# Six attention units with sums of exponentials on TensorE and a three-pass value product, and weight conversion in fewer, wider, moved steps

## The chip, the core and the metric

The kernel runs on one core of a Trainium2 chip. The metric is the device time of one execution in microseconds (us). The core's engines each run their own instruction stream in order and wait for each other through semaphores: PE (TensorE) multiplies matrices, DVE (VectorE), ACT (ScalarE) and POOL (GpSimd) work on rows, and SP issues the transfers. PEld is the loading of PE's stationary operand.

## What is computed

Three layers follow each other on x of shape 8 x 576 x 512. The change touches the first and the way in which weights of the second are prepared.

```python
def _attn_ref(q, k, v, phi):            # 8 batches, 8 heads, 576 rows, 64 columns, 32 memory slots
    a = phi - np.max(phi, axis=2, keepdims=True)
    a = np.exp(a)
    a = a / (np.sum(a, axis=2, keepdims=True) + 1e-09)
    k_m = np.einsum('bhsm,bhsd->bhmd', a, k)
    v_m = np.einsum('bhsm,bhsd->bhmd', a, v)
    scores = scale * np.matmul(q, k_m.transpose(0, 1, 3, 2))
    scores = scores - np.max(scores, axis=-1, keepdims=True)
    attn = np.exp(scores)
    attn = attn / (np.sum(attn, axis=-1, keepdims=True) + 1e-09)
    return np.matmul(attn, v_m)
def _moe_ref(x, w_tok1, w_tok2, w_ch1, w_ch2):
    xt = x.transpose(0, 2, 1)
    h = np.maximum(xt @ w_tok1, 0.0) @ w_tok2
    u = x + h.transpose(0, 2, 1)
    return u + np.maximum(u @ w_ch1, 0.0) @ w_ch2
```

A third layer (gated attention by four experts) ends the program. The weights `w_tok1`, `w_tok2`, `w_ch1`, `w_ch2` arrive as 64-bit floats.

## The kernel before

Products are made in three passes of fp32r matmuls: each operand is split into a high and a low part, and `mm3` adds high times high, high times low, and low times high. Plain fp32 matmuls (transposes, `s2k`, `s3`) stand as two records each in the trace.

**Units.** The attention layer and the token half of the second layer run in 16 units n (a batch and four of its heads), spread over a loop t = -3 to 15, so that in one turn unit t is in its last steps (`s4a`, `s4g`, `s4b`, `s4c`), unit t+1 in its scores (`s3`, `s3b`, `s3c`), unit t+2 in its memory products (`s2s`, `s2k`, `s2t`, `s2q`) and unit t+3 in its first softmax (`s1a`, `s1t`, `s1b`). `s2s` adds up the exponentials of a unit over its five row blocks on POOL (tile `es`); `s2k` multiplies them with keys and values (20 matmuls with 32-column weights, four heads side by side in the array), and one more matmul of `es` with a column of ones gives the sums over the partitions. `s2k` then builds `Vh` and `Vl`, the high and low values of four heads on a masked diagonal, and on POOL and ACT the doubled tile `Vd`, which holds each half of them twice. `s4a` transposes the attention weights and splits them into `aT` in four pieces of 64 partitions, high part of one pair of heads beside its low part; with the doubled values two matmuls then do what three passes do. `s4c` uses them, at 288 columns each, and adds the token product. DVE's `hl` of `s4b` (L435) follows the last matmul of `s4b`; its start is used as a mark of a unit below.

**Blocks.** From t = 2 on, PE's stream is filled up with the first three of twelve column blocks of the channel product (`block_1`, tiles `b`, `uh`, `ul`, `hh`, `hl`, `u`), 11 pieces for each turn.

**Weight conversion.** `f64_split` turns 64-bit words into a high and a low fp32r tile. For one piece that is ACT L119, DVE L120, L123, L124, L125, L127, ACT L128 and DVE L129. In the loop the pieces are the token weights (nine, 256 or 288 columns), three column blocks of the channel weights (six pieces of 512 columns, staging tiles `cst` of four buffers), and four more column blocks (`more_weights`, 16 pieces of 256 columns, two buffers). A second lot of ten 512-column pieces (`chload`) follows beside the last pieces of `block_1` and the first blocks of the channel stage (tiles `h`, `o`, `hh`, `hl` of L606 and L607).

**Order.** The framework schedules the instructions: it takes the written order as a wish and places each instruction on its engine by a timeline of its own. So the `wsome(w)` calls in the loop do not fix where a conversion step ends up.

Of the kernel before, what the change touches and what calls it, by code (L numbers as in the profile page):

```python
# [8 lines left out]
F32 = mybir.dt.float32  # L9
F32R = mybir.dt.float32r  # L10
I32 = mybir.dt.int32
AF = mybir.ActivationFunctionType
OP = mybir.AluOpType
AX = mybir.AxisListType
# [47 lines left out]
def fused_kernel(ctx: ExitStack, tc, q, k, v, phi, w_tok1, w_tok2, w_ch1, w_ch2,  # L62
# [26 lines left out]
    ones = consts.tile([128, 1], F32, name="ones")  # L89
# [20 lines left out]
    def f64_split(pool, stage, hi, lo, n, wd=512, nb=3):  # L110

        P = stage.shape[0]
        L, Hw = stage[:, :, 0], stage[:, :, 1]
        x = pool.tile([128, wd], I32, name="cx", bufs=nb)
        y = pool.tile([128, wd], I32, name="cy", bufs=nb)
        m = pool.tile([128, wd], F32, name="cm", bufs=nb)
        x_, y_, m_ = x[0:P, 0:n], y[0:P, 0:n], m[0:P, 0:n]

        ACT.activation(m_, Hw.bitcast(F32), AF.Abs, scale=REBIAS)  # L119
        DVE.tensor_scalar(m_, m_, LEAST, MOST, op0=OP.max, op1=OP.min)  # L120
        yield

        DVE.tensor_single_scalar(y_, L, 28, op=OP.logical_shift_right)  # L123
        DVE.tensor_scalar(y_, y_, 0.5, 7.0, op0=OP.mult, op1=OP.min)  # L124
        DVE.scalar_tensor_tensor(x_, m_.bitcast(I32), 3, y_, op0=OP.logical_shift_left, op1=OP.bitwise_or)  # L125
        yield
        DVE.scalar_tensor_tensor(y_, Hw, SIGN, x_, op0=OP.bitwise_and, op1=OP.bitwise_or)  # L127
        ACT.activation(hi, y_.bitcast(F32), AF.Copy)  # L128
        DVE.tensor_sub(lo, y_.bitcast(F32), f(hi))  # L129
        yield  # L130
# [69 lines left out]
    with ExitStack() as sa:  # L200
# [27 lines left out]

        units = [(b, g) for b in range(B) for g in range(2)]
        NU = len(units)  # L230
        et, kmT, Vh, Vl, ah, al, pmc, est, kst, ssb, aTt, gt_, ht, pmx, Vd = ({} for _ in range(15))

        def load_phi(n):
# [48 lines left out]
                load_phi(n + 2)  # L282

        def s2s(n):
            e = et[n]
            es = wk_.tile([128, 4, M], F32, name="es", bufs=1)
            e2 = wk_.tile([128, 4, 2, M], F32, name="es2", bufs=1)
            est[n] = es
            POOL.tensor_add(e2[:], e[:, :, 0:2, :], e[:, :, 2:4, :])
            POOL.tensor_add(es[:], e[:, :, 4, :], e2[:, :, 0, :])  # L290
            POOL.tensor_add(es[:], es[:], e2[:, :, 1, :])

        def s2k(n):
            e = et.pop(n)
            kv = kv_
            es = est.pop(n)
            p = pp.tile([128, 512], F32, name="g", bufs=2)
            for j in range(5):
                for h in range(4):
                    PE.matmul(p[32 * h:32 * h + 32, 0:128], lhsT=e[:, h, j, :],  # L300
                              rhs=kv[:, :, h, j, :], start=(j == 0), stop=(j == 4),
                              tile_position=(0, 32 * h))
            PE.matmul(p[:, 128:129], lhsT=es[:].rearrange("p h m -> p (h m)"), rhs=ones[:],
                      start=True, stop=True)
            r = wk_.tile([128, 1], F32, name="kr", bufs=2)
            DVE.tensor_scalar_add(r[:], p[:, 128:129], 1e-9)
            DVE.reciprocal(r[:], r[:])
            ks = wk_.tile([128, 2, 64], F32, name="ks", bufs=1)
            kst[n] = ks
            DVE.scalar_tensor_tensor(ks[:], p[:, None, 0:64].to_broadcast([128, 2, 64]), r[:],  # L310
                                     kmask[:], op0=OP.mult, op1=OP.mult)
            vm = wk_.tile([128, 64], F32, name="vm", bufs=1)
            ACT.activation(vm[:], p[:, 64:128], AF.Copy, scale=r[:])
            if n + 1 < NU:
                load_kv(n + 1)
            vmb = vm[:, None, :].to_broadcast([128, 4, 64])
            h_ = wk_.tile([128, 4, 64], F32R, name="Vh", bufs=3)
            l_ = wk_.tile([128, 4, 64], F32R, name="Vl", bufs=3)
            Vh[n], Vl[n] = h_, l_
            vh = wk_.tile([128, 64], F32R, name="vh", bufs=1)  # L320
            vl = wk_.tile([128, 64], F32, name="vl", bufs=1)
            POOL.tensor_copy(vh[:], vm[:])
            POOL.tensor_sub(vl[:], vm[:], f(vh[:]))
            POOL.tensor_mul(h_[:], f(vh[:])[:, None, :].to_broadcast([128, 4, 64]), vmask[:])
            POOL.tensor_mul(l_[:], vl[:, None, :].to_broadcast([128, 4, 64]), vmask[:])
            d_ = wk_.tile([128, 2, 4, 64], F32R, name="Vd", bufs=3)
            Vd[n] = d_
            for i, x in enumerate((h_, l_)):
                for c, o in ((0, 0), (1, 64)):
                    cs = slice(2 * c, 2 * c + 2)  # L330
                    POOL.tensor_copy(d_[o:o + 64, i, cs, :], f(x[o:o + 64, cs, :]))
                    ACT.activation(d_[64 - o:128 - o, i, cs, :], f(x[o:o + 64, cs, :]), AF.Copy)
# [62 lines left out]
        def s4a(n):  # L395
# [7 lines left out]
            PE.transpose(p2[:], a_[:, 4, :], ident[:])  # L403

            for src, cs, j in ((p[:], slice(0, 512), 4), (p2[:, 0:ST], slice(512, S), 1)):
                for c, o in ((0, 0), (1, 64)):
                    sv = src[o:o + 64, :].rearrange("k (j p) -> k p j", j=j)
                    hv = x_[o:o + 64, c, cs].rearrange("k (p j) -> k p j", j=j)
                    lv = x_[64 - o:128 - o, c, cs].rearrange("k (p j) -> k p j", j=j)
                    split(hv, lv, sv)  # L410
# [27 lines left out]
        def s4c(n):  # L438
# [5 lines left out]
            for c in range(2):  # L444
                cs = slice(128 * c, 128 * c + 128)
                u_ = u1[b][:, 2 * g + c, :]
                for hf in range(2):
                    ss = slice(SH * hf, SH * hf + SH)
                    pu = pp.tile([128, 512], F32, name="g", bufs=2)[:, 0:SH]
                    for i in range(2):  # L450
                        PE.matmul(pu, lhsT=d_[:, i, 2 * c:2 * c + 2, :].rearrange("p h d -> p (h d)"),
                                  rhs=x_[:, c, ss], start=(i == 0), stop=False)
                    mm3(pu, [((hh[:, t, cs], hl[:, t, cs]), (t2h[:, t, ss], t2l[:, t, ss])) for t in range(2)],
# [31 lines left out]

        def more_weights(spool):
            for fc in range(N1, N1 + NP):
                yield from ch_weights(wbm, spool, fc, 256, 2)

        wl = all_weights()  # L490

        def wsome(k):
            for _ in range(k):
                next(wl, None)

        load_phi(0)
        load_kv(0)
# [13 lines left out]
                next(blocks, None)  # L511

        for t in range(-3, NU):
            w = (1, 2, 1, 2, 2)[t] if t < 2 else t % 2
            if t == 2:
                for _ in wl:
                    pass
# [7 lines left out]
            fill(2)  # L525
            on(s3, t + 1)
            on(s2s, t + 2)
            wsome(w)
            fill(1)
            on(s4g, t)  # L530
            on(s1t, t + 3)
            on(s3b, t + 1)
            fill(1)
            on(s2k, t + 2)
            wsome(w)
            fill(1)
            on(s4b, t)
            on(s2q, t + 2, 0)
# [1 line left out]
            fill(1)  # L540
            on(s1b, t + 3)
            on(s3c, t + 1)
            wsome(w)
            c4 = on(s4c, t)
            for i in range(4):
                if c4:
                    next(c4)
                if i == 0:
                    on(s2t, t + 2)
                    on(s2q, t + 2, 2)  # L550
                fill(1 if i else 2)
                wsome(w)
            if c4:
                for _ in c4:
                    pass
# [606 lines left out]
```

## Time and profile before

| | before |
|---|---|
| median of 3 runs (lowest to highest) | 1266.99 us (1263.14 to 1268.27) |
| the profiled execution | 1266.63 us, span 1264.7 us |
| PE busy | 1203.1 us (95%) |
| DVE busy | 740.7 us (59%) |
| ACT busy | 608.7 us (48%) |
| POOL busy | 399.3 us (32%) |

The time of the profiled execution is 1.9 us longer than its span, which reaches from the first instruction to the last. Busy is the share of the span in which an engine had an instruction at work; it is an average over stages in which different engines end last.

### The profile page before, as it was taken

How to read it: one execution, taken by the hardware profiler on the slowest of the kernel's cores; microseconds unless marked ns; L12 is line 12 of the kernel's file. 1: busy time of each engine (PE TensorE's matmuls, PEld its weight loads, DVE VectorE, ACT ScalarE, POOL GpSimd, SP SyncE). 2: the span in 40 equal slices, each digit the busy share in tenths (PEclk: the TensorE clock that was granted, in tenths of full speed). 3: DMA queues.
4: the chain of work that ended last, by engine and by line, in shares of the span. 5: the costliest groups of instructions: out<-in, count | busy, mean ns of one | idle time of the engine just before them, and what ended most of it. 6: DMA issues, size and time to landing. Idle time of an engine off the chain costs nothing. (4 is left out here: it accounts for less than half of the span.)

```text
span 1264.7 us, 22766 instructions
## 1 busy us (share of the span) xinstructions
PE 1203.1 (95%) x8208; PEld 1103.2 (87%) x8208; DVE 740.7 (59%) x1870; ACT 608.7 (48%) x1602; POOL 399.3 (32%) x630
## 2 busy tenths in 40 slices
PE   5698999999999989999999999999999999999997
PEld 4588899999999878888888888999999999998995
DVE  7999966666554782222222123676666766676754
ACT  3565655545454331111111112576676767676775
POOL 2442434334220042000000004363545545373422
PEclk9579999999999999999999999999999999999999
DMA  9755645455414664122210123232323232322421
GB/s 232 209 155 178 193 139 158 130 152 149 123 48 167 224 200 151 36 100 100 100 67 25 43 67 104 71 98 76 80 84 80 76 80 84 113 72 69 135 90 59
DMA packets 160831, 142.91 MB, mean 113 GB/s; under 512 B 73296, under 2 KB 128592, under 8 KB 160720
## 3 DMA queue, kind: packets, MB, share of 16 engines
q1 hardware_dynamic: 160720, 141.47, 38.1%
q8 instruction: 65, 1.06, 0.4%
q14 instruction: 46, 0.38, 0.1%
HBM read 90.05 MB, written 39.85 MB: 103 GB/s over the span
## 5 line engine op out<-in xcount | busy, mean ns | idle before, releaser
L607 DVE SCALAR_TENSOR_TENSOR hl<-h,hh 128x512 fp32r<-128x512 f32 x63 | 43.5, 690 | 225.2 <-ACT hh L606 225.2
L606 ACT ACTIVATE hh<-h 128x512 fp32r<-128x512 f32 x63 | 37.6, 597 | 257.3 <-PE h L97 257.3
L903 POOL TENSOR_TENSOR a<-a,cf 128x128 f32<-128x128 f32 (+3 forms) x128 | 87.9, 719 | 60.6 <-DVE cf L895 49.3
L97 PE MATMUL h<-uh,w1h 128*128 128x512 f32 x252 | 98.8, 393 | 2.2 <-DVE hl L607 2.2
L97 PE MATMUL o<-hl,w2h 128*128 128x512 f32 x252 | 98.4, 390 | 1.0 <-DVE hl L607 1.0
L97 PE MATMUL h<-ul,w1h 128*128 128x512 f32 x252 | 98.5, 391 | 0.0
L97 PE MATMUL h<-uh,w1l 128*128 128x512 f32 x252 | 98.5, 391 | 0.0
L97 PE MATMUL o<-hh,w2l 128*128 128x512 f32 x252 | 98.1, 389 | 0.0
L97 PE MATMUL o<-hh,w2h 128*128 128x512 f32 x252 | 88.6, 389 | 0.0
L847 DVE CUSTOM_DVE_ANT_0 ssb<-s,cmask 128x128 f32<-128x128 f32 (+2 forms) x144 | 69.2, 483 | 31.4 <-PE s L858 20.5
L860 ACT ACTIVATE a<-ssb,nb 128x128 f32<-128x128 f32 (+3 forms) x128 | 71.5, 559 | 13.8 <-DVE nb L847 9.0
L709 POOL MEMSET cmask<- 128x640 f32 x1 | 0.6, 632 | 241.1 <-PE h L97 241.1
L97 PE MATMUL g<-xl,qkh 128*128 128x288 f32 x256 | 76.5, 300 | 0.0
L97 PE MATMUL g<-xh,qkh 128*128 128x288 f32 x256 | 75.8, 301 | 0.0
L97 PE MATMUL g<-xh,qkl 128*128 128x288 f32 x256 | 75.6, 296 | 0.0
L380 POOL TENSOR_TENSOR at<-ssb,ssm 128x640 f32<-128x640 f32 x16 | 20.5, 1279 | 170.6 <-DVE ks L310 113.9
L760 POOL TENSOR_TENSOR xl<-p,xh 128x288 fp32r<-128x288 f32 x64 | 50.7, 806 | 46.6 <-ACT xh L759 46.5
L97 PE MATMUL b<-uh,w1h 128*128 128x288 f32 x192 | 59.1, 309 | 3.7 <-DVE hl L179 2.8
L104 DVE TENSOR_TENSOR Bl<-t,Bh 128x512 fp32r<-128x512 f32 (+1 forms) x80 | 50.5, 635 | 18.8 <-ACT Bh L101 17.6
L97 PE MATMUL b<-hh,w2h 128*128 128x288 f32 x192 | 57.8, 301 | 1.7 <-DVE u L187 1.7
L97 PEld LDWEIGHTS h<-uh,w1h 128*128 128x128 f32 x252 | 47.7, 189 | 12.5 <-DVE hl L607 2.7
L97 PE MATMUL b<-hl,w2h 128*128 128x288 f32 x192 | 58.0, 302 | 0.3 <-DVE hl L179 0.3
(256 smaller groups left out, 4083.1 us busy)
## 6 DMA issues: line engine op xcount, KB each, us to landing
u_d<-u SPq DMA_DIRECT2D x32, 288.0 KB, 2.1
p_d<-u SPq DMA_DIRECT2D x16, 576.0 KB, 3.2
ub<-u_d SPq DMA_DIRECT2D x9, 1024.0 KB, 5.1
pb<-p_d SPq DMA_DIRECT2D x36, 256.0 KB, 3.4
x_d<-pb SPq DMA_DIRECT2D x36, 256.0 KB, 2.2
u<-u_d SPq DMA_DIRECT2D x16, 576.0 KB, 4.1
p<-x_d SPq DMA_DIRECT2D x16, 576.0 KB, 4.1
kv<-in_k_dram SPq DMA_DIRECT2D x16, 512.0 KB, 4.2
```

The source lines that it names most:

```text
L97: PE.matmul(ps, lhsT=a, rhs=b, start=start and i == 0, stop=stop and i == len(seq) - 1)
L104: DVE.tensor_sub(lo, src, f(hi))
L380: POOL.tensor_mul(a_[:].rearrange("p j (h m) -> p j h m", h=4), s[:], sm[:, :, :, None].to_broadcast([128, 5, 4, M]))
L606: ACT.activation(hh[:], p[:], AF.Relu)
L607: DVE.scalar_tensor_tensor(hl[:], p[:], 0.0, f(hh[:]), op0=OP.max, op1=OP.subtract)
L709: POOL.memset(cmask[:], 0.0)
L760: POOL.tensor_sub(xl[b][:, c, ss], x_, f(xh[b][:, c, ss]))
L847: DVE.tensor_tensor_reduce(out=out, in0=p, in1=mask, scale=-scale, scalar=least, op0=OP.add, op1=OP.min, accum_out=acc)
L860: ACT.activation(a[:, aoff[c]:aoff[c] + W], s_[:, 0:W], AF.Exp, scale=-1.0, bias=nb[:, 0:1], accum_out=sm[:, c:c + 1])
L903: POOL.tensor_mul(x_, x_, cf[:, c:c + 1].to_broadcast([128, W]))
```

## The change

It has four parts. (1) For units 0 to 5 (`n < NR`), `s2s` is left out; `s2k` gets the sums from 20 matmuls of the exponentials themselves with the column of ones. (2) For the same units `Vd` is not made; `s4a` splits all 128 partitions at once, high parts in `x_[:, 0]` and low parts in `x_[:, 1]`, and `s4c` makes the three passes with `Vh` and `Vl`. (3) In every conversion L123 and L124 become one instruction that reads the low word as an unsigned number. (4) The pieces of `more_weights` are 512 columns wide in place of 256, eight in place of 16, still with two staging buffers, and the code asks for one step in every third slot from t = 4 on, where it asked for one in every slot of odd turns from t = 3 on.

```diff
-        DVE.tensor_single_scalar(y_, L, 28, op=OP.logical_shift_right)
-        DVE.tensor_scalar(y_, y_, 0.5, 7.0, op0=OP.mult, op1=OP.min)
+        DVE.tensor_scalar(y_, L.bitcast(U32), 2.0 ** -29, 7.0, op0=OP.mult, op1=OP.min)
...
+        NR = 6
...
         def s2s(n):
+            if n < NR:
+                return
...
-            PE.matmul(p[:, 128:129], lhsT=es[:].rearrange("p h m -> p (h m)"), rhs=ones[:],
-                      start=True, stop=True)
+            if n < NR:
+                for j in range(5):
+                    for h in range(4):
+                        PE.matmul(p[32 * h:32 * h + 32, 128:129], lhsT=e[:, h, j, :], rhs=ones[:],
+                                  start=(j == 0), stop=(j == 4), tile_position=(0, 32 * h))
+            else:
+                PE.matmul(p[:, 128:129], lhsT=est.pop(n)[:].rearrange("p h m -> p (h m)"), rhs=ones[:],
+                          start=True, stop=True)
...
+            if n < NR:
+                Vd[n] = h_, l_
+                return
...
             for src, cs, j in ((p[:], slice(0, 512), 4), (p2[:, 0:ST], slice(512, S), 1)):
+                if n < NR:
+                    split(x_[:, 0, cs].rearrange("k (p j) -> k p j", j=j),
+                          x_[:, 1, cs].rearrange("k (p j) -> k p j", j=j),
+                          src.rearrange("k (j p) -> k p j", j=j))
+                    continue
...
-                    for i in range(2):
+                    if n < NR:
+                        ws = [v[:, 2 * c:2 * c + 2, :].rearrange("p h d -> p (h d)") for v in d_]
+                        mm3(pu, [(ws, (x_[:, 0, ss], x_[:, 1, ss]))], stop=False)
+                    for i in range(2 * (n >= NR)):
...
-                yield from ch_weights(wbm, spool, fc, 256, 2)
+                yield from ch_weights(wbm, spool, fc, 512, 2)
...
+        def wsoon():
+            nonlocal wslot
+            wslot += 1
+            if wslot % 3 == 0:
+                next(wl, None)
...
-            w = (1, 2, 1, 2, 2)[t] if t < 2 else t % 2
+            go = (lambda: wsome((1, 2, 1, 2, 2)[t])) if t < 2 else wsoon if t >= 4 else (lambda: None)
```

Every `wsome(w)` in the loop becomes `go()`. How the instructions stand after scheduling is shown at three places. The first is DVE behind the mark of unit 2 (L435 before, L451 in the changed kernel); `ul`, `u` and the `hl` with a number belong to `block_1`. Before:

```order
L435 SCALAR_TENSOR_TENSOR hl<-g,hh 128x512
L123 TENSOR_SCALAR cy<-cst 128x256
L179 SCALAR_TENSOR_TENSOR hl_1233<-b,hh_1232 128x288
L279 TENSOR_TENSOR ea<-phb_112,t 128x640
L104 TENSOR_TENSOR ul_1332<-u_692,uh_1331 128x288
L123 TENSOR_SCALAR cy<-cst 128x256
L104 TENSOR_TENSOR ul_1332<-u_692,uh_1331 128x288
L124 TENSOR_SCALAR cy<-cy 128x256
L104 TENSOR_TENSOR ul_1332<-u_692,uh_1331 128x288 x2
L120 TENSOR_SCALAR cm<-cm 128x256
L124 TENSOR_SCALAR cy<-cy 128x256
```

And in the changed kernel:

```order
L451 SCALAR_TENSOR_TENSOR hl<-g,hh 128x512
L127 SCALAR_TENSOR_TENSOR cy<-cst,cx 128x512
L318 SCALAR_TENSOR_TENSOR ks<-g,kr,kmask 128x128
L129 TENSOR_TENSOR w1l_3527<-cy,w1h_3526 128x512
L179 SCALAR_TENSOR_TENSOR hl_1240<-b,hh_1239 128x288
L105 TENSOR_TENSOR ul_1338<-u_690,uh_1337 128x288 x4
L124 TENSOR_SCALAR cy<-cst 128x512
L121 TENSOR_SCALAR cm<-cm 128x512
L125 SCALAR_TENSOR_TENSOR cx<-cm,cy 128x512
L124 TENSOR_SCALAR cy<-cst 128x512
L127 SCALAR_TENSOR_TENSOR cy<-cst,cx 128x512
```

The pieces of `more_weights` are wide now, and they have not moved back: all eight are done before the mark of unit 3 in the changed order, while in the order before ten narrow pieces begin before that mark and the last ends behind the mark of unit 4.

The second place is PE at `s2k` of unit 3 (`ea` holds the exponentials). Before:

```order
L418 MATMUL g<-t1l,ahi 128x256
L300 MATMUL g<-kv,ea 32x128 x20
L303 MATMUL g<-ones,es 128x1
L267 MATMUL t<-ident,pmx 128x128
L347 MATMUL t<-ident,qn 128x128 x8
```

And in the changed kernel:

```order
L434 MATMUL g<-t1l,ahi 128x256
L268 MATMUL t<-ident,pmx 128x128
L302 MATMUL g<-kv,ea 32x128 x20
L308 MATMUL g<-ones,ea 32x1 x20
L358 MATMUL t<-ident,qn 128x128 x8
```

One full-width matmul has become 20 narrow ones with one column each.

The third place is DVE in the channel stage, between two successive `hl` (L607 before, L634 changed) where the next block's input is split; `ul` from `ub` is the split of the next block's input. Before:

```order
L607 SCALAR_TENSOR_TENSOR hl<-h,hh 128x512
L124 TENSOR_SCALAR cy<-cy 128x512
L104 TENSOR_TENSOR ul<-ub,uh 128x512 x4
L120 TENSOR_SCALAR cm<-cm 128x512
L129 TENSOR_TENSOR w1l_6194<-cy,w1h_6193 128x512
L125 SCALAR_TENSOR_TENSOR cx<-cm,cy 128x512
L127 SCALAR_TENSOR_TENSOR cy<-cst,cx 128x512
L607 SCALAR_TENSOR_TENSOR hl<-h,hh 128x512
```

And in the changed kernel:

```order
L634 SCALAR_TENSOR_TENSOR hl<-h,hh 128x512
L105 TENSOR_TENSOR ul<-ub,uh 128x512 x4
L129 TENSOR_TENSOR w2l_6206<-cy,w2h_6205 128x512
L634 SCALAR_TENSOR_TENSOR hl<-h,hh 128x512
```

Of nine DVE instructions that stood between these two `hl`, five are left; the others stand further forward or are gone.

## Rows read from the trace of the kernel before

**Rows 1.** Windows: length; PE, PEld, DVE, ACT, POOL busy (instructions); PE clock, DMA, GB/s

```profile
22.00:59.70 37.70, 24.17 (x169) 20.54 (x168) 37.21 (x82) 20.29 (x45) 15.03 (x20) 0.68 0.86 225
59.70:129.24 69.54, 60.10 (x499) 56.52 (x500) 65.60 (x148) 40.13 (x105) 25.73 (x40) 0.88 0.58 165
129.24:180.28 51.04, 49.36 (x442) 47.73 (x440) 45.30 (x103) 32.53 (x90) 25.48 (x42) 1.00 0.60 171
```

**Rows 2.** DVE groups by form, 22 to 175 us: count, busy us, mean ns, idle before

```profile
L125 DVE SCALAR_TENSOR_TENSOR cx<-cm,cy 128x256 int32<-128x256 int32 x19 | 10.3, 542 | 0.2
L127 DVE SCALAR_TENSOR_TENSOR cy<-cst,cx 128x256 int32<-128x256 int32 x20 | 10.0, 507 | 0.1
...
L104 DVE TENSOR_TENSOR aT<-t,aT 64x512 fp32r<-64x512 f32 x12 | 8.3, 688 | 0.5 <-ACT aT L101 0.2
L123 DVE TENSOR_SCALAR cy<-cst 128x256 int32<-128x256 int32 x18 | 7.8, 432 | 3.5 <-DMA cst<-in_moe_w_ch_dram 3.4
L124 DVE TENSOR_SCALAR cy<-cy 128x256 int32<-128x256 int32 x18 | 7.4, 409 | 0.1
L120 DVE TENSOR_SCALAR cm<-cm 128x256 f32<-128x256 f32 x18 | 6.1, 340 | 0.2
...
L125 DVE SCALAR_TENSOR_TENSOR cx<-cm,cy 128x512 int32<-128x512 int32 x6 | 5.1, 849 | 0.0
...
L127 DVE SCALAR_TENSOR_TENSOR cy<-cst,cx 128x512 int32<-128x512 int32 x6 | 4.5, 743 | 0.1
...
L124 DVE TENSOR_SCALAR cy<-cy 128x512 int32<-128x512 int32 x6 | 3.7, 621 | 0.0
...
L129 DVE TENSOR_TENSOR w2l<-cy,w2h 128x256 fp32r<-128x256 f32 x8 | 3.6, 451 | 0.0
L120 DVE TENSOR_SCALAR cm<-cm 128x512 f32<-128x512 f32 x6 | 3.0, 496 | 0.0
...
L123 DVE TENSOR_SCALAR cy<-cst 128x512 int32<-128x512 int32 x6 | 2.6, 432 | 0.0
...
L129 DVE TENSOR_TENSOR w1l<-cy,w1h 128x512 fp32r<-128x512 f32 x3 | 2.4, 808 | 0.0
```

**Rows 3.** Timeline of DVE from 450 us: start us, length us, instruction

```profile
452.35 0.68 DVE L127 SCALAR_TENSOR_TENSOR cy<-cst,cx 128x512 int32<-128x512 int32 x1
452.95 0.41 DVE L123 TENSOR_SCALAR cy<-cst 128x512 int32<-128x512 int32 x1
```

**Rows 4.** The staging tile `cst`, 22 to 175 us: durations, smallest, median, largest, ns

```profile
L123 DVE TENSOR_SCALAR cy<-cst x28: 278/300/1365, 23.4 to 154.9; 128x256 int32<-128x256 int32 x18, 128x512 int32<-128x512 int32 x6, 128x288 int32<-128x288 int32 x4
```

**Rows 5.** POOL groups by form, 22 to 175 us

```profile
L289 POOL TENSOR_TENSOR es<-ea 128x256 f32<-128x256 f32 x7 | 6.5, 929 | 27.2 <-ACT kmT L339 13.6 <-ACT ea L280 13.3
```

**Rows 6.** Timeline of PE, one turn in which PE never waits

```profile
235.16 1.30 PE L300 MATMUL g<-kv,ea 128*32 128x128 f32 x40
236.39 0.38 PE L303 MATMUL g<-ones,es 128*128 128x1 f32 x2
236.63 0.38 PE L97 MATMUL b<-uh,w1h 128*128 128x288 f32 x1
236.85 0.30 PE L97 MATMUL b<-ul,w1h 128*128 128x288 f32 x1
236.98 0.29 PE L97 MATMUL b<-uh,w1l 128*128 128x288 f32 x1
```

**Rows 7.** Window of the channel stage, columns as in the first group

```profile
450.00:470.00 20.00, 16.73 (x65) 12.78 (x64) 19.42 (x29) 6.73 (x12) 9.73 (x15) 0.91 0.66 193
```

**Rows 8.** DVE groups by form, 388 to 470 us

```profile
L124 DVE TENSOR_SCALAR cy<-cy 128x512 int32<-128x512 int32 x10 | 5.9, 590 | 0.0
```

**Rows 9.** What PE waited for, 388 to 520 us: total us, times, longest

```profile
PE h L97 <- DVE hl L607: 2.2, 1, 2.2
```

**Rows 10.** DMA issues of the staging tile, 22 to 175 us: count, KB each, us to landing

```profile
cst<-in_moe_w_ch_dram SPq DMA_DIRECT2D x16, 256.0 KB, 3.1
cst<-in_moe_w_ch_dram SPq DMA_DIRECT2D x6, 512.0 KB, 4.5
```

More of the change, by code (lines that the diff above doesn't have):

```diff
@@ L11 @@
 I32 = mybir.dt.int32
+U32 = mybir.dt.uint32
 AF = mybir.ActivationFunctionType
@@ L295, in s2k @@
             kv = kv_
-            es = est.pop(n)
             p = pp.tile([128, 512], F32, name="g", bufs=2)
@@ L494, in wsome @@
                 next(wl, None)
+        def wsoon():
[3 more added lines that the diff above has]
+                next(wl, None)
+        wslot = 0
         load_phi(0)
@@ L527, in fused_kernel @@
             on(s2s, t + 2)
-            wsome(w)
+            go()
             fill(1)
@@ L534, in fused_kernel @@
             on(s2k, t + 2)
-            wsome(w)
+            go()
             fill(1)
@@ L542, in fused_kernel @@
             on(s3c, t + 1)
-            wsome(w)
+            go()
             c4 = on(s4c, t)
@@ L551, in fused_kernel @@
                 fill(1 if i else 2)
-                wsome(w)
+                go()
             if c4:
```

## The prediction

> **What bounds the kernel now.** I read first the windows of the stretches that the change touches, cut at the marks of the units (the start of L435). From 22 us to the mark of unit 0 DVE is busy 37.2 of 37.7 us, and from there to the mark of unit 3, at 129.24 us, 65.6 of 69.5 us, while PE is idle for 69.5 - 60.1 = 9.4 us [rows 1]. So DVE ends last up to the mark of unit 3. From there to the first transposes of unit 6, at 180.28 us, PE is busy 49.4 of 51.0 us and DVE 45.3: the bound has gone over to PE, which idles for 1.7 us [rows 1]. Behind 180 us nothing of the first two parts is left, and PE works through the remaining units and blocks without a gap. The clock column matters as well: 0.68 and 0.88 of full speed in the first two stretches, 1.00 in the third [rows 1], so PE has spent part of its time there at the lower of its two levels.
>
> Then the groups of DVE by form, because DVE is what has to become shorter: they give the mean length of each instruction of a conversion, at 256 and at 512 columns, and of the split of `aT` [rows 2]. Last I looked for other places that hold conversions: the ten pieces beside the start of the channel stage. There DVE is busy 19.4 of the 20 us from 450 on, PE is idle for 20 - 16.7 = 3.3 us, and the clock is 0.91 [rows 7]; one wait of 2.2 us is for DVE's `hl` of L607 [rows 9].
>
> **DVE up to the mark of unit 3.** The two orders show which instructions stand ahead of that mark. Gone are 25 of L124: 19 narrow ones (four of them of 288 columns, which I take at the narrow mean) and six wide ones, 19 x 0.409 + 6 x 0.621 = 11.5 us [rows 2]. Gone with the narrow pieces are ten each of L120, L123 and L125, nine of L127 and eight of L129: 3.40 + 4.32 + 5.42 + 4.56 + 3.61 = 21.3 us. New are eight wide pieces, each 0.496 + 0.432 + 0.849 + 0.743 + 0.808 = 3.33 us, together 26.6 us [rows 2]. This is more than goes, as all eight (the work of 16 narrow ones) now stand ahead of the mark. Four units save one 512-column `aT` split each, 4 x 0.688 = 2.8 us, and a short one of 64 columns that I leave out. Net: 11.5 + 21.3 + 2.8 - 26.6 = 9.0 us. Lengths of neighbours overlap in the records: an L127 of 0.68 us is followed after 0.60 us [rows 3]. Some 40 instructions fewer at such overlaps would give back 2 to 3 us; the small split and the short waits around it give part of that back, so I take 8.
>
> The new instruction of (3) is in no trace. It reads `cst` with the stride of L123 and does arithmetic like L124, so it lies between L123 (0.432 us at either width) and a wide L124 (0.621) [rows 2]. I take L123, since it is the reading that they share; at the other end eight wide and some 15 other pieces would lose 23 x 0.19 = 4.4 us.
>
> **POOL's part.** L123 takes anything from 278 to 1365 ns at nearly equal sizes [rows 4], so something holds it up. Units 0 to 5 lose three POOL additions (the first is 0.93 us [rows 5]) and four copies. If all of what lies above the shortest form vanished, L123 alone would gain 18 x (0.432 - 0.278) = 2.8 us. But most POOL work stays. I take 2 us for all forms together, with 0 and 5 as ends.
>
> The Trainium skill (SBUF — State Buffer, Who interferes with whom) says that DVE and GpSimd share one port pair, and that an instruction which takes it blocks the other engine for its whole length. The spread of L123 agrees with it. By that rule the sum would go to the far end, 5 us in place of 2; it is taken up under the rivals.
>
> **PE.** The three passes add four 288-column matmuls to a unit, at 0.13 us from start to start [rows 6]: 0.5 us. The sums are 20 fp32 matmuls, 40 records. The nearest row is the 40 records of keys and values with the same 32-column weights, which take 1.23 us; the two records that go take 0.24 [rows 6]. I take 1.2 - 0.2 = 1.0 us for a unit. The lower end is nothing; the upper is the step of the single matmul, 0.12 us for each of 40 records, 4.8 us. The Trainium skill (TensorEngine Tiling (Array Packing), Performance Considerations) speaks against this part: a matmul has about 60 cycles of overhead and one with a free size of 1 lasts as long as one with 60. By that rule 40 records are 2400 cycles, by estimate 1.0 us at 2.4 GHz and 2.0 us at the lower level; no run here shows it yet.
>
> Between the marks of units 0 and 3 PE gets three units of this: 12 x 0.13 + 3 x 1.0 = 4.6 us, and loses about 7 block matmuls that move behind the mark, 0.9 us. Of its 9.4 us of slack 5.7 remain, and DVE's gain in that stretch must fit in there; the gain ahead of 59.7 us, 3 of the 8 us by the two orders, needs none of it. So 10 us of DVE's gain (8 + 2) would leave both engines full, which a chain between two engines does not reach: I give 2.5 us to new waits. **The mark of unit 3 comes 7.5 us earlier.**
>
> From there PE sets the pace. It gets ten matmuls of `s4c` and seven block matmuls more before unit 6, 17 x 0.13 = 2.2 us. Of its 1.7 us idle time I give back 1.0, since DVE has no conversions left there. The stretch becomes 51.0 + 2.2 - 1.0 us, and unit 6 begins 7.5 - 1.2 = 6.3 us earlier. Behind it four matmuls are left, 0.3 us: **6 us** remain.
>
> What is taken off ACT (four copies and two short splits for each unit) and POOL shortens no end: ACT is busy 40 of 69.5 us in the second stretch, POOL 26 [rows 1].
>
> **The ten pieces beside the channel stage.** Each loses an L124 of 0.59 us, 5.9 us together [rows 8], from a DVE that is all but full [rows 7]. The wait of 2.2 us [rows 9] stands behind four `ul` and four steps of conversions; the changed order leaves four `ul` and one step there. I count the idle 3.3 us as gone. The clock of 0.91 means 2 x 0.09 x 20 = 3.6 us at the lower level, which cost half of that, 1.8 us. At most 5.1 us can come back; I take **4 us**, as other waits of a few tenths will show up; the lower end is nothing.
>
> Sum, against the profiled execution: 1266.6 - 6 - 4 = 1256.6 us. This run stands 0.4 us below the median, so the same number serves for the median.
>
> **The rivals.** *The gain in the units is eaten by PE* (0.18). If each set of sums costs 2 us or more, PE's added work in the second stretch is 1.6 + 6 - 0.9 = 6.7 of the 9.4 us, and the mark of unit 3 can move by hardly more than 3 (ahead of 59.7) + 2.7; with waits 4, less 1.5 later, leaves 2.5. Then 1266.6 - 2.5 - 4 = 1260 us. For it: the clock of 0.88. Against it: kv's 40 records at 1.23 us.
>
> *The channel stage gains nothing* (0.13), because the order of PE there changes too and a new wait takes the place of the old: 1266.6 - 6 = 1260.6 us.
>
> *More than that* (0.10): POOL's part is 5 us, and PE, with shorter pauses, stays at the full clock. The 0.88 of 69.5 us is 16.7 us at the lower level, which cost up to 8 us. Then DVE alone is the bound to the mark of unit 3, which moves by 8 + 5 - 1 = 12 us: 1266.6 - 12 + 1.5 - 4.6 = 1251.5 us.
>
> *Slower* (0.06): the wide pieces wait for their transfers. There are two staging buffers, and a 512 KB load lands 4.5 us after its issue where a 256 KB one took 3.1 [rows 10]; DVE already waits for them, 3.5 us ahead of the narrow L123 [rows 2]. DVE runs in order, so `aT`, `gl` and `hl`, for which PE waits, stand behind a piece whose data is late. In the changed order the sixth and the eighth piece, which share a buffer, are some seven instructions apart, about 3.4 us by their means: a wait of 1.5 to 2 us there, as much as goes with the narrow ones. If five pieces waited for a whole landing, that would be 22 us: 1266.6 + 22 - 10 = 1278.6 us. It decides from 10 us of such waits on. Against it: the other pieces' buffers are free 5 us or more ahead.
>
> *Part (4) does not do what its text says*: the steps are not later but earlier in the order. That is already in the sum, as DVE's load before the mark.
>
> **How the numbers follow.** The likeliest case, 0.53, is both gains at about these sizes, 1252 to 1260.5. The range from 1250 to 1264 takes in the two half gains and the larger one, and leaves out the slower case and the far ends. A change under 0.5%, some 6 us, is hardly told from none in this kernel, so "faster" means below 1260.7: most of the first case, all of the larger gain, and less than half of the two half gains, 0.70. Same: 0.24. Slower: 0.06.
>
> **What would show it.** The mark of unit 3 near 122 us, that of unit 0 near 56; the first transposes of unit 6 near 174. In the window up to the mark of unit 3 both PE and DVE above 90%. The new L124 at about 0.43 us, with no row at the length of the old pair. The 40 records of sums at about 1.2 us where PE does not wait. No wait of PE for `hl` above 1 us near 460 us and a clock of 1.0 there. It would be wrong if PE's wait for DVE in the units stays although DVE has less to do, if DVE waits longer than 5 us in all for `cst` between the marks of units 1 and 3, or if the last stage, from 800 us on, which no part touches, changes by more than 2 us.

## The result, and the profile after

The changed kernel takes 1255.78 us in the median of four runs (1255.56 to 1257.66); the kernel before, 1267.63 us in the runs beside it. The ratio is 0.9917, with an interval of 0.9891 to 0.9943: some 10.5 us less by the ratio (the two medians lie 11.9 us apart), where the prediction had 1256.6 us. The span of the profiled execution went from 1264.7 to 1253.9 us.

First the marks. These are the two rows of the last `hl` group of the channel stage, before (L607) and after (L634): how many, shortest, median and longest in ns, then the start of the first and of the last.

```profile
L607 DVE SCALAR_TENSOR_TENSOR hl<-h,hh x63: 677/691/692, 416.6 to 762.2; 128x512 fp32r<-128x512 f32 x63
```

```profile
L634 DVE SCALAR_TENSOR_TENSOR hl<-h,hh x63: 673/692/692, 409.4 to 750.0; 128x512 fp32r<-128x512 f32 x63
```

So the channel stage begins 7.2 us earlier and is left 12.2 us earlier. All of the second difference arises by the tenth `hl`, which starts at 473.9 us before and at 461.6 us after: 5.1 us come from the ten pieces there. These are the windows from the first to the tenth `hl`, before and after, columns as in [rows 1]:

```profile
416.60:473.90 57.30, 54.02 (x249) 44.61 (x248) 44.84 (x76) 18.67 (x32) 17.88 (x24) 0.97 0.63 197
```

```profile
409.40:461.60 52.20, 51.66 (x246) 43.10 (x246) 40.37 (x65) 18.36 (x32) 15.31 (x21) 1.00 0.59 184
```

From the last `hl` to the end it is 502.5 us before and 503.9 after. So the profiled gain is 7.2 + 5.1 (less 0.1 in between) - 1.4 = 10.8 us. Of the 7.2 us, 5.7 arise ahead of the mark of unit 0 (59.7 to 54.0 us), only 0.6 between that mark and the mark of unit 3, and the rest behind it.

The windows after, columns as in [rows 1], cut at the marks of unit 0 and 3 and at the transposes of unit 6; then the stretch from the mark of unit 2 to that of unit 3, and the place of [rows 7]:

```profile
22.00:54.02 32.02, 22.17 (x236) 18.61 (x235) 30.94 (x72) 17.11 (x37) 5.79 (x7) 0.73 0.91 248
54.02:122.89 68.87, 61.29 (x625) 59.12 (x626) 60.14 (x117) 36.35 (x85) 21.67 (x26) 0.88 0.73 198
122.89:172.44 49.55, 49.55 (x451) 48.83 (x450) 29.37 (x59) 25.48 (x68) 19.86 (x34) 1.00 0.54 145
96.59:122.89 26.30, 26.30 (x253) 26.07 (x254) 20.04 (x43) 11.87 (x29) 6.25 (x11) 0.89 0.65 188
450.00:470.00 20.00, 19.55 (x85) 15.91 (x86) 9.55 (x14) 2.74 (x5) 6.44 (x12) 1.00 0.65 198
```

DVE's load up to the mark of unit 3 fell from 102.8 [rows 1] to 91.1 us, that of POOL from 40.8 to 27.5. But PE is full from the mark of unit 2 on, 26.30 of 26.30 us, one unit earlier than the prediction had it, and DVE idles there for 6 us. Near 460 us PE is all but full, DVE half empty, and the clock, 0.91 before, is 1.00.

The new instruction of part (3) in DVE's groups, 22 to 166.8 us, beside which [rows 2] had the pair of L123 and L124:

```profile
L124 DVE TENSOR_SCALAR cy<-cst 128x512 int32<-128x512 uint32 x14 | 6.4, 459 | 2.2 <-DMA cst<-in_moe_w_ch_dram 2.1
```

It takes 459 ns at 512 columns, near the 432 of L123 and not the 621 of the old L124. DVE waits 2.1 us in all for the staged channel weights.

The sums on TensorE, in the timeline of PE (start, length in us), where [rows 6] had only the narrow kv product and one wide matmul:

```profile
115.97 0.62 PE L302 MATMUL g<-kv,ea 128*32 128x128 f32 x16
116.40 0.54 PE L308 MATMUL g<-ones,ea 128*32 128x1 f32 x40
116.88 0.40 PE L98 MATMUL b<-uh,w1h 128*128 128x288 f32 x1
```

The 40 records take 0.48 us, from 116.40 to 116.88, not 1.2.

### The profile page after: what moved, and what is told of

The parts are those of the page before. It is cut to its first block, busy times and chain, and to the rows that moved or that the text cites. A ratio compares the mean times of both kernels' runs of the same rounds, so it can differ in the third digit from the quotient of the medians.

```text
span 1253.9 us, 23043 instructions
## 1 busy us (share of the span) xinstructions
PE 1204.2 (96%) x8460; PEld 1108.1 (88%) x8460; DVE 710.2 (57%) x1777; ACT 595.1 (47%) x1550; POOL 377.2 (30%) x588
## 5 line engine op out<-in xcount | busy, mean ns | idle before, releaser
L634 DVE SCALAR_TENSOR_TENSOR hl<-h,hh 128x512 fp32r<-128x512 f32 x63 | 43.5, 690 | 224.4 <-ACT hh L633 224.4
L946 PE MATMUL t<-ident,a 128*128 128x128 f32 x320 | 56.0, 280 | 1.9 <-DVE Al L105 1.2
```

Of the source, the lines that this page charges most:

```text
L634: DVE.scalar_tensor_tensor(hl[:], p[:], 0.0, f(hh[:]), op0=OP.max, op1=OP.subtract)
L946: PE.transpose(p[:, 128 * kc:128 * kc + 128], a[:, aoff[c] + 128 * kc:aoff[c] + 128 * kc + 128], ident[:])
```

## The experiments

Theory A in the expectations is the prediction's own account: DVE's instruction count first, 2 us from POOL, the sums and third passes a price on PE. P is what I held after the first four runs: that POOL's work slows DVE, and that PE is the bound from the mark of unit 2 on. The medians carry a disturbance: the last stage, in which none of these kernels differ, took between 502.5 and 506.6 us in their profiles. So differences under 4 us are read from the profiled marks, which stand ahead of that stage: the start of `s4b`'s `hl` of unit 3 (mark 3) and of the channel stage's last `hl`.

Two things limit such readings. Each kernel was profiled once, so how far a mark scatters between executions is not known, and differences of 1 or 2 us are hints. And PE's granted clock between the marks of units 0 and 3 is not the same in all kernels (column "clock"): 0.06 less over some 67 us is 2 x 0.06 x 67 = 8 us at the lower level, by estimate up to 4 us for a full PE. So a mark carries a kernel's clock as well as its work.

| kernel | median us | ratio to before, interval | mark 3 | last `hl` | clock |
|---|---|---|---|---|---|
| before | 1265.98 to 1267.63 | 1 | 129.2 | 762.2 | 0.88 |
| changed | 1255.78 | 0.9917 (0.9891 to 0.9943) | 122.9 | 750.0 | 0.88 |
| part (3) alone | 1255.86 | 0.9911 (0.9894 to 0.9929) | 124.1 | 750.4 | 0.92 |
| without part (3) | 1256.50 | 0.9923 (0.9903 to 0.9944) | 121.9 | 750.3 | 0.94 |
| without part (4) | 1253.26 | 0.9896 (0.9877 to 0.9916) | 121.5 | 748.9 | 0.88 |
| four units | 1251.71 | 0.9879 (0.9861 to 0.9897) | 119.8 | 746.1 | 0.90 |
| 16 units | 1260.69 | 0.9962 (0.9947 to 0.9977) | 121.8 | 755.0 | 0.88 |
| POOL's work back | 1259.26 | 0.9948 (0.9932 to 0.9964) | 125.0 | 751.7 | 0.84 |
| part (1) alone | 1266.91 | 1.0003 (0.9992 to 1.0013) | 130.5 | 763.5 | 0.90 |
| part (2) alone | 1259.79 | 0.9950 (0.9934 to 0.9967) | 121.8 | 755.5 | 0.93 |
| four units, without (4) | 1254.80 | 0.9909 (0.9894 to 0.9924) | 119.2 | 745.9 | 0.93 |
| without part (1) | 1257.79 | 0.9927 (0.9915 to 0.9940) | 125.0 | 751.7 | 0.88 |
| three units, without (4) | 1254.54 | 0.9905 (0.9892 to 0.9919) | 121.0 | 747.2 | 0.88 |
| work in PE's pauses | 1251.92 | 0.9876 (0.9859 to 0.9892) | 118.7 | 745.2 | 0.94 |

**Part (3) alone**, on the kernel before:

```diff
-        DVE.tensor_single_scalar(y_, L, 28, op=OP.logical_shift_right)
-        DVE.tensor_scalar(y_, y_, 0.5, 7.0, op0=OP.mult, op1=OP.min)
+        DVE.tensor_scalar(y_, L.bitcast(U32), 2.0 ** -29, 7.0, op0=OP.mult, op1=OP.min)
```

> The kernel before with part (3) alone: L123 and L124 as one instruction, in all 39 and 10 pieces. Theory A (DVE's load decides up to the mark of unit 3, and any 10 us taken off DVE there serve as well as any other): DVE loses 11.5 us ahead of the mark of unit 3, PE gets nothing added and has 9.4 us of slack, so the marks move by 6 to 8 us, the channel stage gives its 4.5, together 1255 to 1257 us, the same as the changed kernel. Rival B (the parts for the six units carry the gain there): the units give 2 to 3 us, the channel stage 4.5, 1260 us.

It took 1255.86 us: one instruction fewer in each conversion brings as much as all four parts. The mark of unit 3 comes 5.1 us earlier, and the stretch from the first to the tenth `hl` of the channel stage is 50.7 us long (before 57.3), with PE busy in all of it. The time is the one that Theory A gave; its two halves are not, 5.1 us where it had 6 to 8 and 6.6 beside the channel stage where it had 4.5.

**The changed kernel without part (3)**: the reverse of this edit.

> The changed kernel with L123 and L124 apart again, parts (1), (2) and (4) kept. Theory A: DVE gets 11 us back ahead of the mark of unit 3 and 5.9 us beside the channel stage, so the waits near 460 us are back and the marks stand within 2 us of those before: 1265 to 1269 us. Rival B: the units keep 4 to 5 us and only the channel stage is lost, 1262 us.

It took 1256.50 us; every expectation was missed, by 5 us or more. In the channel stage the account holds by half: DVE is busy 44.5 us between the two `hl` (40.4 in the changed kernel) and PE idles 2.5 us, but 2.5 of the 5.1 us are gained all the same, with a clock of 1.00 there. And the units gain 9.3 us up to the first `hl` of the channel stage, without the instruction that was to bring most of it. By the scheduled order 56064 columns of conversion instructions stand ahead of mark 3, where the kernel before has 47616, and still that mark is 7.3 us earlier. What differs from before is that wide pieces do more columns in an instruction, that the half splits are gone, that POOL has 26.1 us of work instead of 40.8, and that PE's clock is higher between the marks of units 0 and 3:

```profile
54.60:121.90 67.30, 59.98 (x633) 57.16 (x634) 63.80 (x130) 37.83 (x87) 20.35 (x23) 0.94 0.70 197
```

That is 2 x 0.06 x 67.3 = 8.1 us at the lower level, where the changed kernel has 2 x 0.12 x 68.87 = 16.5: up to 4 us for a full PE. The six runs of this kernel had a mean clock of 0.989 to 0.997 over their whole length, the four of the changed one 0.982 to 0.989. So this run does not show what part (3) is worth in the set at an equal clock. Three DVE groups of this kernel, 22 to 121.9 us:

```profile
L128 DVE SCALAR_TENSOR_TENSOR cy<-cst,cx 128x512 int32<-128x512 int32 x13 | 11.1, 852 | 0.0
L126 DVE SCALAR_TENSOR_TENSOR cx<-cm,cy 128x512 int32<-128x512 int32 x13 | 8.9, 688 | 0.0
...
L125 DVE TENSOR_SCALAR cy<-cy 128x512 int32<-128x512 int32 x14 | 6.2, 441 | 0.0
```

The same three were 743, 849 and 621 ns before [rows 2]: one is longer, two are shorter. By the means of all its forms a wide piece takes DVE 3.7 us here and took 3.9. That the quieter POOL is the cause is not shown by these rows; what POOL alone does is measured below.

**Without part (4)**, and **four units** in place of six:

```diff
-                yield from ch_weights(wbm, spool, fc, 512, 2)
+                yield from ch_weights(wbm, spool, fc, 256, 2)
...
-            go = (lambda: wsome((1, 2, 1, 2, 2)[t])) if t < 2 else wsoon if t >= 4 else (lambda: None)
+            go = lambda: wsome((1, 2, 1, 2, 2)[t] if t < 2 else t % 2)
```

> The changed kernel without part (4): more_weights in 16 narrow pieces and in the old slots, parts (1) to (3) kept. Theory A: ahead of the mark of unit 3 DVE has ten narrow pieces in place of eight wide ones, about 5 us less, of which PE's slack lets through 2 at most, and six narrow pieces, 11 us, lie behind the mark, where DVE has room; within 2 us of the changed kernel, 1254 to 1258 us. Rival C (the wide pieces are what helps, by fewer fixed costs): 3 to 5 us slower than the changed kernel, 1259 to 1261 us.

```diff
-        NR = 6
+        NR = 4
```

> The changed kernel with NR = 4 in place of 6, so that units 4 and 5 are as before. Theory A with PE as the bound behind the mark of unit 2: PE loses 2 x 4 matmuls of 0.13 us in s4c of units 4 and 5 and two sets of 40 records for 2 of about 0.12, 2 x (0.5 + 1.0) = 3 us, of which the set of unit 4 may lie in a wait; 1253 to 1255 us. Rival D (DVE still decides up to unit 5): its splits and POOL's copies come back there, and the time is equal or up to 2 us longer.

Without part (4) the last `hl` is 1.1 us earlier, not later: the wide pieces bring nothing in this set. With four units it is 3.9 us earlier, and the time, 1251.71 us, lies below both expectations. Its window from the mark of unit 2 to that of unit 3, to be held against 96.59 to 122.89 above:

```profile
97.70:119.80 22.10, 22.10 (x202) 21.74 (x202) 20.52 (x44) 13.04 (x32) 8.31 (x13) 0.98 0.67 202
```

PE is full in both; it has some 50 records less, and a clock of 0.98 for 0.89. The lower level held 2 x 0.11 x 26.3 = 5.8 us of the one window and 2 x 0.02 x 22.1 = 0.9 us of the other, and so, by estimate, cost 2.5 us more in the one. Of the other 1.7 us the sums of unit 5 are 0.24. The rest is order: ten matmuls of `block_1` (seven now ahead of the mark of unit 2, where PE still pauses, and three behind mark 3) and three of `s4c` stand elsewhere, 1.6 us at 0.12. Behind mark 3, where units 4 and 5 have eight matmuls less, it is 286.4 us to the first `hl` of the channel stage after 286.5: what they save there goes to matmuls that moved in. So the gain is not the two units' work alone.

**Parts (1) and (2) for all units**, the ten in which PE has no idle time among them:

```diff
-        NR = 6
+        NR = 16
```

> The changed kernel with parts (1) and (2) for all 16 units instead of six. In units 6 to 15 TensorE has no idle time, so that what the sums and the third pass cost there must show in full. By the lengths measured in the changed kernel (40 records of sums 0.48 us less 0.24 us, four matmuls of 0.13 us) a unit costs 0.8 us, ten units 8 us: about 1263 to 1264 us. By the prediction's price (1.0 and 0.5 us) it is 15 us: about 1271 us. If a unit with more TensorE work gains as much from less work on the other engines, the time stays at 1256.

The windows from the mark of unit 6 to that of unit 15, of this kernel and then of the changed one:

```profile
188.60:386.10 197.50, 197.50 (x2022) 196.27 (x2021) 98.35 (x216) 78.47 (x206) 39.48 (x55) 1.00 0.42 121
```

```profile
189.40:381.30 191.90, 191.90 (x1719) 189.38 (x1718) 112.34 (x234) 96.56 (x255) 62.28 (x108) 1.00 0.44 124
```

This stretch is 5.6 us longer, for nine third passes but only seven sets of sums, since those of units 6 to 8 stand ahead of it. From mark 3 to the first `hl` of the channel stage, where all ten units' work stands and PE is full, it is 293.0 against 286.5 us: 0.65 us a unit, for sums and third passes together. The sum of the single lengths was 0.8, the prediction's 1.5; the time, 1260.69 us, is below the 1263 that the single lengths gave.

**POOL's work put back.** The changed kernel, in which `s2s` runs for units 0 to 5 again and nobody reads its result; the orders of PE, DVE and ACT are the same to the instruction.

```diff
         def s2s(n):
-            if n < NR:
-                return
...
+                est.pop(n)
```

> The changed kernel, but GpSimd does the three additions of s2s for units 0 to 5 again, and nobody reads them; nothing else changes. Theory P (what GpSimd lost is a large part of the gain, since VectorE is slowed while GpSimd works): the mark of unit 3 comes 4 to 7 us later than in the changed kernel, and the time is 1259 to 1262 us where TensorE doesn't hide it. Theory A of the prediction (VectorE's instruction count counts, GpSimd's relief is 2 us): the mark moves by 2 us at most, 1256 to 1258 us.

Its windows, 22 us to the mark of unit 0 and on to that of unit 3:

```profile
22.00:54.90 32.90, 22.35 (x240) 18.68 (x239) 31.76 (x69) 16.22 (x35) 9.81 (x13) 0.72 0.94 249
54.90:125.00 70.10, 63.07 (x623) 61.32 (x624) 61.29 (x117) 36.03 (x85) 28.08 (x35) 0.84 0.67 188
```

POOL has 10.4 us more, and DVE is busy 93.05 instead of 91.1 us, with three instructions fewer in the windows. One form by itself, up to mark 3:

```profile
L124 DVE TENSOR_SCALAR cy<-cst 128x512 int32<-128x512 uint32 x14 | 7.8, 556 | 1.3 <-DMA cst<-in_moe_w_ch_dram 1.3
```

It was 459 ns. Mark 3 is 2.1 us later and the last `hl` 1.7; the ratio rose by 0.0031, 3.9 us, and the profiled last stage is 1.1 us longer. So POOL's three additions are worth 2 us of the marks: the size that the prediction took for additions and copies together, not the 4 to 7 that I had come to expect, though the time lies where Theory P had it.

**Part (1) alone** and **part (2) alone**, each on the kernel before, with `NR = 6` and these lines of the change and no others. Part (1):

```diff
         def s2s(n):
+            if n < NR:
+                return
...
+            if n < NR:
+                for j in range(5):
+                    for h in range(4):
+                        PE.matmul(p[32 * h:32 * h + 32, 128:129], lhsT=e[:, h, j, :], rhs=ones[:],
+                                  start=(j == 0), stop=(j == 4), tile_position=(0, 32 * h))
```

> The kernel before with part (1) alone: sums of six units on TensorE, no additions on GpSimd there. VectorE's instructions are those of before. Theory P: GpSimd's relief alone brings the mark of unit 3 forward by 4 to 6 us, 1261 to 1263 us. Theory A: 2 us from GpSimd, less 0.24 us on TensorE for a unit: 1265 to 1267 us, no difference that can be measured.

Part (2):

```diff
+            if n < NR:
+                Vd[n] = h_, l_
+                return
...
+                if n < NR:
+                    split(x_[:, 0, cs].rearrange("k (p j) -> k p j", j=j),
+                          x_[:, 1, cs].rearrange("k (p j) -> k p j", j=j),
+                          src.rearrange("k (j p) -> k p j", j=j))
+                    continue
...
+                        mm3(pu, [(ws, (x_[:, 0, ss], x_[:, 1, ss]))], stop=False)
```

> The kernel before with part (2) alone: three passes of the value product in six units, without doubled values. VectorE loses a 512-column split for a unit, 2.8 us up to the mark of unit 3; GpSimd's work stays nearly whole; TensorE gets 0.5 us for a unit. Theory A: 2 to 3 us less up to the mark of unit 3, 1 to 2 us of it given back behind: 1264 to 1266 us. Theory P the same, as GpSimd keeps its additions; if this part alone brings 5 us or more, neither theory holds and what counts is that the split no longer writes two halves by separate instructions ahead of the value product.

Their windows from the mark of unit 0 to that of unit 3, part (1) first:

```profile
57.20:130.50 73.30, 61.84 (x622) 58.17 (x623) 68.37 (x156) 43.22 (x112) 25.05 (x36) 0.90 0.59 160
```

```profile
58.20:121.80 63.60, 58.67 (x510) 55.16 (x511) 58.72 (x136) 33.45 (x86) 22.68 (x31) 0.93 0.62 175
```

Part (1) alone changes nothing. DVE does 237 instructions from 22 us to mark 3 in 102.5 us, where the kernel before did 229 in 102.8: they are shorter on average, but by the orders 1792 more columns of conversion stand ahead of the mark. That this eats the relief is read from the orders and was not tried. Part (2) alone brings 6.7 us up to the last `hl`, more than either theory gave it. DVE's load up to mark 3 falls by 8.5 us, of which its splits (eight of 688 and eight of 216 ns become four of each length) are 3.6; POOL's falls from 40.8 to 33.5 us as well, and PE idles 4.9 instead of 9.4 us between the marks, at a clock of 0.93 instead of 0.88. What makes up the rest of DVE's 8.5 us was not tried.

**The parts recombined**: four units without part (4), which is the two short edits above together; the changed kernel without part (1); three units without part (4). The edit of the second:

```diff
         def s2s(n):
-            if n < NR:
-                return
...
-            if n < NR:
-                for j in range(5):
...
-            else:
-                PE.matmul(p[:, 128:129], lhsT=est.pop(n)[:].rearrange("p h m -> p (h m)"), rhs=ones[:],
-                          start=True, stop=True)
+            PE.matmul(p[:, 128:129], lhsT=est.pop(n)[:].rearrange("p h m -> p (h m)"), rhs=ones[:],
+                      start=True, stop=True)
```

> The changed kernel with NR = 4 and without part (4): narrow pieces in the slots of before. Theory P (from mark 2 on TensorE is full, so what counts there is its own work, and where the pieces stand doesn't): mark of unit 3 near 120 us as with four units alone, 1250 to 1253 us. If the two small gains seen singly add up (2.5 us without part (4), 4 us with four units), 1249 us. If narrow pieces in the old slots hold VectorE up once TensorE has less to do there, 1254 us or more.

> The changed kernel without part (1): GpSimd adds up the exponentials again and TensorE has one matmul for the sums; parts (2), (3) and (4) stay. Theory P (GpSimd's relief by part (1) is worth the 3.5 to 4 us that its work cost when it was put back unread, less 0.5 us for each unit's sums on TensorE, which count from unit 2 on): 1256.5 to 1258.5 us. Theory S (part (1) is worth nothing in the set either, as it was alone): 1254 to 1256 us.

> As with four units and the old slots, but NR = 3: unit 3 has its sums, its doubled values and its two half splits as before. TensorE gets 0.8 us less work where it is full, VectorE 0.9 us and GpSimd about 3 us more up to the mark of unit 3. If TensorE alone sets the end from mark 2 on: 0.5 to 1 us less than with four units. If the two are about even there: 1 to 3 us more.

Four units without part (4) end the channel stage where four units with it do (745.9 and 746.1 us). Their medians differ by 3.1 us, but so do the last stages, 506.6 and 503.9; so mark 3 is where Theory P had it and the time, 1254.80 us, is not, and nothing is read from it. Without part (1) the last `hl` is 1.7 us later, as far as with POOL's work put back. But the way there is another (mark 0 at 56.5 and 54.9 us, a clock of 1.00 and 0.89 between marks 2 and 3), and the interval of its ratio overlaps that of the changed kernel; that part (1) is worth 1.7 us in the set, all of it POOL's, is not shown. With three units the last `hl` is 1.3 us later than with four, and the medians lie 0.3 us apart. The kernel with three falls behind between the marks of units 1 and 2, 20.8 against 17.6 us, with DVE idle for 6.6 of the 20.8 us, PE for 1.0, and a clock of 0.84 against 1.00. So the work that went back to DVE and POOL is not seen to decide there.

**Work in PE's pauses.** The changed kernel with 24 fp32 matmuls that nobody reads, in the turns in which PE waits most:

```diff
+            if n < 3:
+                d_ = ppb1.tile([128, SH], F32, name="b", bufs=2)
+                for i in range(8):
+                    PE.matmul(d_[:, 0:128], lhsT=ident[:], rhs=e[:, 0, 0:4, :], start=True, stop=True)
```

> The changed kernel with eight more matmuls of 128x128 fp32, whose result nobody reads, behind the sums of units 0, 1 and 2, where TensorE idles; at the 0.28 us of the transposes they are 6.7 us of work. Theory K (the lower clock ahead of 103 us, 34 us in all, costs several us, and more work in the pauses keeps the clock up): less than 20 us at the lower clock up to the mark of unit 3, and that mark 1 to 4 us earlier, 1252 to 1255 us. Theory P (the clock is a consequence of the pauses and the chain between the engines sets these marks): the lower clock stays within 7 us of its length, or its loss brings nothing, and the mark of unit 3 is 1 to 5 us later, 1257 to 1261 us.

Its windows between the marks of units 0, 1, 2 and 3, and below them the first two of the changed kernel, whose third is the row 96.59:122.89 above:

```profile
56.20:77.00 20.80, 18.35 (x196) 17.56 (x197) 20.29 (x43) 11.92 (x27) 6.43 (x5) 0.89 0.66 198
77.00:94.40 17.40, 14.66 (x184) 13.98 (x183) 17.01 (x32) 10.88 (x26) 7.75 (x8) 1.00 0.83 223
94.40:118.70 24.30, 24.30 (x248) 24.10 (x247) 22.86 (x49) 13.98 (x33) 5.15 (x8) 0.93 0.69 209
```

```profile
54.00:77.20 23.20, 19.98 (x192) 18.94 (x193) 22.30 (x41) 12.24 (x28) 8.02 (x8) 0.78 0.69 182
77.20:96.60 19.40, 15.02 (x184) 14.13 (x183) 17.83 (x36) 12.24 (x28) 7.41 (x9) 0.97 0.88 230
```

The mark of unit 0 is 2.2 us later, and then 2.4, 2.0 and 2.0 us come back: mark 3 is 4.2 us earlier, and the time is 1251.92 us. In the first of the three stretches the time at the lower level (1.2 GHz) went from 10.2 to 4.6 us, which would be worth 2.8 to a full PE; but there DVE is all but full in both kernels (22.30 of 23.20 and 20.29 of 20.80 us), and its own load fell by the 2.0 us. In the third, where PE is full, it went from 5.8 to 3.4, worth 1.2 by estimate. The second has nearly the same clock in both kernels (1.00 and 0.97), but by the scheduled orders 1536 columns of conversion less. So the clock's share is 1.2 us at least and 4 at most of the 6.4 us, the rest another order. The expectation of less than 20 us at the lower level was missed: from 22 us to mark 3 it was 24.6, after 33.8.

## Why the prediction came out right

The forecast was 10 us, 6 in the units and 4 beside the channel stage; measured are 7.2 and 5.1, less 1.4 in the last stage. By its steps:

- **DVE up to the mark of unit 3**: 8 us by count and 2 from POOL; its load fell by 11.7, and more than half of that, 6.3, ahead of the mark of unit 0 (37.21 to 30.94 us), where the sum had 3 of the 8. Of the 11.7, POOL's relief was measured at 2 us by one part; what the four copies of part (2) did to DVE was not measured by itself.
- **New waits**, 2.5 us: 5.4, since mark 3 moved by 6.3 and not by 11.7. This is the step with the largest error, and the windows show its place: most of DVE's added idle time stands between the marks of units 2 and 3, 6.3 us where it had been 1.8, and there PE is full. PE, not DVE, sets the pace from the mark of unit 2 on, where the prediction had it change over at unit 3. Kernels with fewer matmuls or a higher clock in that stretch (four units, work in the pauses) reach mark 3 earlier by 3 to 4 us; part (3) added to (1), (2) and (4) comes with a mark 1 us later, but with a lower clock too.
- **PE's price**, 1.5 us for a unit: the term was mis-sized, 0.65 us where PE is full. The sums were priced by kv's row, 1.0; the records show 0.48 less 0.24. It entered the sum only through the slack that it left to DVE, and so through the waits.
- **Behind the mark of unit 3**, 1.2 us longer: 1.5 us shorter. Of the 17 matmuls that I added there, nine more records are in the trace, with 0.2 us more busy time, and the idle 1.7 us went whole. (The four matmuls counted behind unit 6 would be 0.5 us at 0.13, not 0.3.)
- **The ten pieces beside the channel stage**, 4 us: 5.1. The merged kernels that were profiled take 50.7 to 52.2 us for that stretch and those without part (3) 54.7 to 57.3. Its mechanism is shown by part (3) alone; its removal from the set gives back 2.5 of the 5.1 us, while the clock stays at 1.00 (0.97 before).
- **What was to be seen**: marks near 56 (54.0), 122 (122.9) and 174 (172.4), the new L124 near 0.43 (0.46), no wait near 460 us, the last stage within 2 us: right. PE and DVE above 90% up to mark 3: wrong, 89 and 87%, because the two take turns, DVE all but full up to the mark of unit 1 (22.30 of 23.20 us), and PE behind that of unit 2. One sign of being wrong came true for the most part: PE's waits for DVE ahead of mark 3, 17.4 us before, are still 15.6, the longest for `ks` (6.0) and `hl` (3.9).

Of the rivals, *eaten by PE* fell with the price of the sums; *the channel stage gains nothing* with its 5.1 us; *slower* with 2.1 us of waits for the staged channel weights where 10 would decide. *More than that* names a reserve: 1251.92 us, near its 1251.5, was reached by another edit with a clock of 0.94 in place of 0.88, and without its 5 us from POOL, so that the nearness of the two numbers is luck. And *part (4) is not what its text says* holds, and more: in this set it brings nothing.

What the prediction did not see is that the gains of its parts do not add up. Part (3) alone gives 11.8 us by the last `hl`, (1), (2) and (4) together 11.9, all of them 12.2. Part (3) takes 6 us from DVE up to mark 3 (34.95 + 61.80 busy against 102.8) and adds nothing to PE; the other three take 6.6 from DVE and add 6 x 0.65 = 3.9 us to PE. Together they unload an engine that, from the mark of unit 2 on, is no longer waited for. The clock differs between these kernels (0.88, 0.92 and 0.94 between marks 0 and 3), so how much of the missing sum is due to it stays open. That the total came out right is partly luck: the waits were 2.9 us more than forecast and the last stage took 1.4, against 1.7 us more off DVE, 2.7 us better behind mark 3 and 1.1 beside the channel stage.

The best two kernels, four units (1251.71 us) and work in the pauses (1251.92 us), are each about 4 us ahead of the changed one, with intervals that just touch its own. Both edits act on PE. The two together were not tried.

## What to carry to other kernels

When several edits unload the same engine, ask after each of them which engine ends last, and in which unit; here one instruction fewer in a conversion was worth as much as the whole set. Look at the clock of each kernel before a difference is put down to its work. A part that buys time on the unloaded engine with work on the next bound should stop where the bound changes over: four units ended the channel stage earlier than six and sixteen, and three were not better. Price a new small instruction by its own nearest form, the number of columns it moves, and not only by its weights.

## What the hardware showed that was not expected

- 40 fp32 records of one column, with four 32-column strips side by side, took 0.48 us, 12 ns a record, where 40 records of 128 columns took 1.2. The Trainium skill (TensorEngine Tiling (Array Packing), Performance Considerations) has some 60 cycles of overhead for each matmul; by that rule it would be, by estimate, 1.0 us. The measurement decides: less than half.
- 10.4 us more of POOL's work lengthened DVE's by 2 us in an unchanged order, and one form from 459 to 556 ns. The Trainium skill (SBUF — State Buffer, Who interferes with whom) says that the two share a port pair; the trace agrees, at a fifth of POOL's time.
- The lower clock cost next to nothing ahead of the mark of unit 0, where DVE is the bound: 0.98 without part (4) and 0.73 in the changed kernel, marks at 53.5 and 54.0 us. Between the marks of units 2 and 3, where PE is full, the changed kernel's 5.8 us at the lower level are, by estimate, 2.9 us.
- The last stage took 502.5 to 506.6 us with the same instructions, and its length goes with the time at the lower clock: by the traces' clock records 0.2 us of it before (502.5 us), 4.7 in the changed kernel (503.9), 8.1 to 8.4 in four others (505.0 to 505.6) and 11.3 in two (505.9 and 506.6). These stretches stand at other places in each kernel. What sets them stays open.
